# Moving one transposed load behind the first unpacking copies, and splitting four tiles' work on the fourth weight piece

## The chip, the cores and the metric

The kernel runs on one core of one Trainium2 chip. The metric is the device time of one launch in microseconds (us); the time before is the median of three runs.

## The reference

`x` is 16 x 512 x 1024, `w` 1024 x 1024 and `b` 1024, all bf16. Every group of four consecutive rows of `w` keeps, column by column, the elements whose magnitude is at least the second largest of the four; the others become zero. Then the pruned matrix is applied.

```
wg = w.reshape(G, M, D)                      # G = 256 groups, M = 4 rows each
mag = jnp.abs(wg)
order = jnp.argsort(mag, 1)
thr = jnp.take_along_axis(mag, order[:, M - N:M - N + 1, :], 1)     # N = 2
wp = (wg * (mag >= thr)).reshape(D, D)
return jnp.einsum("bsd,df->bsf", x, wp) + b
```

## The kernel before

The 8192 tokens are 64 tiles of 128. Tiles 0 to 6 are "packed": they are multiplied while the weights are still being pruned. Tiles 7 to 13 are "filling" tiles: they keep the matrix engine (PE) busy while later weights are pruned. Tiles 14 and 15 are one small batch, and tiles 16 to 63 run in six batches of eight through a regular loop (L373).

The weights are loaded so that partition p of half g holds the four rows of one group, which is what VectorE (DVE) needs to prune. They come in six pieces: pieces 0 to 3 are 256-column quarters of half g = 0, and pieces 4 and 5 are the two 512-column halves of g = 1. The packed tiles use half 0 in that grouped layout directly, against x tiles whose columns were taken apart in the same way (`xT`, by transposes on PE). Every other tile uses x transposed in natural order, and so needs the pruned weights rearranged into `wp_nat`: four copies from on-chip memory to on-chip memory for each half g and each column half h (`unpack`, L176), all issued from the SyncE queue (SP).

The order of the front part is written out by hand in the string `FRONT`. Each token is one step, and every engine and queue works through its own steps in exactly this order. The tokens that matter here:

- `I.1.0.512`, `I.1.512.1024`: load the two column halves of weight half g = 1 (L71, 512 KB each, SP). The loads of pieces 0 to 3 stand ahead of `FRONT`; pieces 2 and 3 come as one load of 512 KB, `load_w(0, 512, 1024)`.
- `D.0`, `D.1`: `load_fill`, the transposing DMA of the filling tiles' x for half 0 or 1 into `xfill` (L263, SP). `G` (L328) is the same for the packed tiles' half 1, into `xg1`. `L.n` (L275) are the transposing loads of the later batches.
- `U.g.h...`: the four unpacking copies of half g, column half h (L176, SP).
- `A.i`, `P.i`: magnitudes of weight piece i (L120 on DVE; piece 3 on ScalarE, L117), and its pruning on DVE (L133 to L153). Pieces 0 to 3 are masked and pruned in two steps, rows m = 0, 1 of each group first and then m = 2, 3.
- `T.t`, `C.t`: transpose packed tile t on PE, copy the result to `xT` on ScalarE (ACT).
- `M.i.t`: the four matmuls (m = 0 to 3) of piece i for packed tile t (L207). `N.i.t.a.b` does only those of the rows a and b that it names, so that work can start when the first half of a piece is pruned.
- `V.h.t`: ACT copies a finished bank to `stage` (L239). `O.h.t`: DVE adds the second half (L243).
- `X.0.t`: four matmuls of filling tile t on half g = 0, 512 columns wide (L207, reading `xfill` and `wp_nat`). `X.0.7` is the first one, and the first reader of what `D.0` and `U.0.0.0.512` bring. `N.4...` after it need `G` and `U.1.0.0.512`; `X.2...` need `D.1`.

Eight accumulator banks are handed out in turn. Each DMA signals one of eight completion semaphores, also in turn, and waits for the earlier user of that semaphore to have landed.

Of the kernel before, what the change touches and what calls it, by code (L numbers as in the profile page):

```python
# [10 lines left out]
def kernel(  # L11
# [8 lines left out]
    P = 128  # L20
# [7 lines left out]
    B, S, D = x.shape  # L28
# [10 lines left out]
    T, F = 7, 7  # L39
# [230 lines left out]
    def issue_batch(t0, nb):  # L270
# [16 lines left out]


    FRONT = """
        I.1.0.512 D.0 A.0 P.0 W W W W W W W W W w w T.0 T.1 C.0 T.2 T.3 C.1 T.4 C.2 N.0.0.0 N.0.0.1 T.5  # L290
        N.0.1.0 N.0.1.1 N.0.0.2 N.0.0.3 N.0.1.2 N.0.1.3 M.0.2 A.1 C.3 P.1 U.0.0.0.512 I.1.512.1024 G C.4 C.5
        M.0.3 N.0.4.0.1 T.6 C.6 N.0.4.2.3 A.2 M.0.5 M.0.6 P.2 N.1.0.0.1 N.1.1.0.1 A.3
        N.1.2.0.1 N.1.0.2.3 N.1.1.2.3 N.1.2.2.3 V.0.0 M.1.3 V.0.1 M.1.4 V.0.2 M.1.5 M.1.6 V.0.3 V.0.4
        P.3 N.2.0.0.1 V.0.5 N.2.1.0.1 N.2.2.0.1 N.2.3.0.1 N.2.0.2.3 V.0.6 N.2.1.2.3 N.2.2.2.3 N.2.3.2.3 M.2.4 M.2.5 M.2.6 A.4 P.4
        U.1.0.0.512 D.1 N.3.0.0.1 N.3.1.0.1 N.3.0.2.3 V.1.0 N.3.1.2.3 M.3.2 V.1.1 M.3.3 V.1.2 M.3.4 V.1.3 M.3.5 V.1.4
        M.3.6 V.1.5 X.0.7 V.1.6 X.0.8 V.0.7 X.0.9 V.0.8 X.0.10 V.0.9 X.0.11 V.0.10 X.0.12 V.0.11 X.0.13 V.0.12 V.0.13
        A.5 P.5 U.1.1.0.512 U.0.1.0.512 Q L.0 L.1 N.4.0.0 N.4.1.0 N.4.2.0 N.4.3.0 N.4.0.1 N.4.1.1 N.4.2.1
        N.4.3.1 N.4.0.2 N.4.1.2 N.4.2.2 N.4.3.2 N.4.0.3 N.4.1.3 N.4.2.3 N.4.3.3 M.4.4 O.0.0 M.4.5 O.0.1
# [109 lines left out]
```

## Time and profile before

| what | us |
|---|---|
| median of 3 runs (233.39 to 233.41) | 233.39 |
| profiled execution, whole | 234.25 |
| its span in the profile | 232.4 |
| PE busy | 227.2 (98%) |
| VectorE busy | 120.4 (52%) |
| ScalarE busy | 17.1 (7%) |
| regular loop L373 on the closing chain | 72% of the span |
| L207 (packed and filling tiles) on the closing chain | 12% of the span |
| granted TensorE clock | 1.0 |

The span starts with the first instruction of the profiled execution; all times below are microseconds from there. 1.85 us of the profiled execution lie outside the span, and that execution is 0.86 us longer than the median. "Busy" of PE counts pipelined matmuls that overlap: one 256-column matmul is recorded as 273 ns, while the next starts 109 ns after it. DMA shares are the mean busy share of the core's 16 DMA engines; they exceed 1 where packets overlap.

### The profile page before, as it was taken

The page shows a single profiled execution, that of the slowest core. Times are in us where ns is not written, and L with a number is a line of the kernel's source. Part 1 is how long each engine was busy: PE and PEld are TensorE (multiplying, and loading weights), DVE is VectorE, ACT ScalarE, POOL GpSimd, SP SyncE. Part 2 cuts the span into 40 slices and gives each one's busy share as a digit, 9 for nine tenths or more (in the row PEclk, how much of TensorE's full clock was granted, in tenths as well). Part 3 has the DMA queues.
Part 4 walks back from the last instruction along what each step waited for, and adds up shares of the span by engine and source line. Part 5 has one row for each costly group of instructions (what it writes and reads, how often), then busy time and mean ns, then how long its engine had stood idle before and what let it go on. Part 6 is the DMA issues. An engine that isn't in the chain of part 4 may idle for free.

```text
span 232.4 us, 2743 instructions
## 1 busy us (share of the span) xinstructions
PE 227.2 (98%) x1123; PEld 110.3 (47%) x1143; DVE 120.4 (52%) x214; ACT 17.1 (7%) x31; POOL 0.7 (0%) x6
## 2 busy tenths in 40 slices
PE   8989999999999999999999999999999999999995
PEld 4876444444444444444444444444444444444443
DVE  4899987777996244234334334324424424423434
ACT  3677500000000000000000000000000000000000
POOL 1000000000000000000000000000000000000000
DMA  6989999999846203992239922597228991122222
GB/s 212 236 187 206 222 234 177 249 249 305 303 181 258 103 26 112 238 253 97 93 101 206 234 92 93 109 233 199 90 93 175 162 278 36 73 90 90 90 90 93
DMA packets 77612, 38.19 MB, mean 164 GB/s; under 512 B 63648, under 2 KB 69408, under 8 KB 77600
## 3 DMA queue, kind: packets, MB, share of 16 engines
q1 hardware_dynamic: 67952, 20.88, 46.7%
q10 hardware_dynamic: 9648, 17.14, 20.4%
q8 instruction: 9, 0.15, 0.3%
q14 instruction: 3, 0.02, 0.0%
HBM read 3.28 MB, written 16.78 MB: 86 GB/s over the span
## 4 chain that ended last, share of the span: by engine, by line
PE 90%; DVE 3%; DMA 3%; SPq 1%; issue 1%
PE bank L373 72%; PE bank L207 12%; PE bank L267 6%; DMA w<-in_w_dram 3%; SPq L79 1%; DVE w L153 1%; DVE mask L150 1%; SPq L71 0%; DVE o_last L358 0%; DVE hi L133 0%; DVE lo L134 0%; DVE thr L143 0%; DVE mag L120 0%; DVE t L141 0%; DVE t L137 0%
## 5 line engine op out<-in xcount | busy, mean ns | idle before, releaser
L373 PE MATMUL bank<-wp_nat,xTb 128*128 128x512 bf16 x737 | 161.7, 379 | 0.8
L252 DVE TENSOR_TENSOR o_pair<-bank,bias_sb 128x512 bf16<-128x512 f32 x105 | 68.0, 687 | 101.2 <-PE bank L373 95.4
L373 PEld LDWEIGHTS <-xTb 128*128 128x128 bf16 x752 | 73.6, 98 | 88.7
L243 DVE TENSOR_TENSOR stage<-bank,stage 128x512 f32<-128x512 f32 x21 | 13.7, 688 | 2.9 <-PE bank L207 2.8
L207 PE MATMUL bank<-w,xT 128*128 128x256 bf16 x112 | 13.3, 273 | 0.8 <-DVE w L153 0.8
L247 DVE TENSOR_TENSOR o_pair<-stage,bias_sb 128x512 bf16<-128x512 f32 x21 | 13.5, 683 | 0.0
L207 PE MATMUL bank<-wp_nat,xfill 128*128 128x512 bf16 x55 | 12.4, 379 | 0.1
L267 PE MATMUL bank<-wp_nat,xfill 128*128 128x512 bf16 x55 | 12.2, 379 | 0.1
L207 PE MATMUL bank<-wp_nat,xg 128*128 128x512 bf16 x54 | 12.1, 380 | 0.1
L207 PEld LDWEIGHTS <-xT 128*128 128x128 bf16 x112 | 10.7, 98 | 2.7 <-issue 1.1
L239 ACT COPY stage<-bank 128x512 f32<-128x512 f32 x21 | 11.0, 609 | 4.2 <-PE bank L207 4.1
L267 PEld LDWEIGHTS <-xfill 128*128 128x128 bf16 x56 | 5.5, 98 | 6.6
L207 PEld LDWEIGHTS <-xg 128*128 128x128 bf16 x56 | 5.5, 98 | 6.6 <-issue 0.2
L207 PEld LDWEIGHTS <-xfill 128*128 128x128 bf16 x56 | 5.5, 98 | 6.4
L373 PE MATMUL bank<-wp_nat,xTs 128*128 128x512 bf16 x32 | 7.1, 379 | 0.0
L153 DVE TENSOR_TENSOR w<-w,mask 128x512 bf16<-128x512 bf16 (+2 forms) x11 | 5.9, 546 | 0.3
L150 DVE TENSOR_TENSOR mask<-mag,thr 128x512 bf16<-128x512 bf16 (+2 forms) x11 | 5.9, 543 | 0.2
L105 PE MATMUL bank<-const-bfloat16-1.0 128*128 128x512 bf16 (+1 forms) x11 | 4.2, 572 | 0.8 <-PEq L392 0.8
L373 PEld LDWEIGHTS <-xTs 128*128 128x128 bf16 x32 | 3.1, 98 | 3.8
L120 DVE TENSOR_SCALAR mag<-w 128x512 uint16<-128x512 uint16 (+2 forms) x6 | 2.7, 469 | 3.1 <-DMA w<-in_w_dram 3.0
L191 ACT COPY xT<-bank 128x512 bf16<-128x512 bf16 x7 | 3.6, 609 | 2.9 <-PE bank L186 2.9
L267 PE MATMUL bank<-wp_nat,xTb 128*128 128x64 bf16 (+3 forms) x39 | 3.6, 248 | 0.1
(20 smaller groups left out, 27.1 us busy)
## 6 DMA issues: line engine op xcount, KB each, us to landing
out_dram<-o_pair ACTq DMA_DIRECT2D x25, 512.0 KB, 3.6
out_dram<-o_pair ACTq DMA_DIRECT2D x13, 256.0 KB, 3.2
wp_nat<-w SPq DMA_DIRECT2D x16, 128.0 KB, 3.1
w<-in_w_dram SPq DMA_DIRECT2D x3, 512.0 KB, 7.1
xh<-in_x_dram SPq DMA_DIRECT2D x3, 128.0 KB, 4.0
xh<-in_x_dram ACTq DMA_DIRECT2D x1, 256.0 KB, 3.9
xh<-in_x_dram SPq DMA_DIRECT2D x1, 256.0 KB, 3.4
w<-in_w_dram SPq DMA_DIRECT2D x1, 256.0 KB, 4.2
```

Of the source, the lines that this page charges most:

```text
L105: K(nc.tensor.matmul(bank[7][:, :n], lhsT=ones[:, :P], rhs=ones[:, :n], start=True, stop=True))
L120: K(nc.vector.tensor_single_scalar(mag[:, ms].bitcast(u16), w_of(i)[:, ms].bitcast(u16), 0x7FFF, op=Alu.bitwise_and))
L150: K(nc.vector.tensor_tensor(mask[:, ms, c], mag[:, ms, c], tb, op=Alu.is_ge))
L153: K(nc.vector.tensor_tensor(w_of(i)[:, ms, c], w_of(i)[:, ms, c], mask[:, ms, c], op=Alu.mult))
L191: K(nc.scalar.copy(xt[:], src))
L207: K(nc.tensor.matmul(dst, lhsT=lhs, rhs=rhs, start=c0 == 0 and m == 0, stop=c1 == FH and m == 3))
L239: K(nc.scalar.copy(stage[(h, t)][:], bank[own[(h, t)]][:]))
L243: K(nc.vector.tensor_tensor(st, bank[own[(2 + h, t)]][:], st, op=Alu.add))
L247: K(nc.vector.tensor_tensor(get_o(t)[:, f], stage.pop((h, t))[:], bias_sb[:, f], op=Alu.add))
L252: K(nc.vector.tensor_tensor(get_o(t)[:, f], bank[bk][:], bias_sb[:, f], op=Alu.add))
L267: K(nc.tensor.matmul(bank[bk][:, :c1 - c0], lhsT=xN[t][:, kt, :], rhs=wp_nat[h][:, kt, c0:c1], start=kt == 0, stop=kt == KT - 1))
L373: K(nc.tensor.matmul(bank[bks[h]][:], lhsT=xN[t][:, kt, :], rhs=wp_nat[h][:, kt, :], start=kt == 0, stop=kt == KT - 1))
```

## The change

Two edits in `FRONT`; nothing else in the kernel differs. `D.0` goes from second place to a place behind `U.0.0.0.512`. For packed tiles 2 and 3 the fourth piece (i = 3) is split: the first-half matmuls of both go ahead of every second-half matmul of that piece, as those of tiles 0 and 1 already did.

```diff
-        I.1.0.512 D.0 A.0 P.0 W W W W W W W W W w w T.0 T.1 C.0 T.2 T.3 C.1 T.4 C.2 N.0.0.0 N.0.0.1 T.5
-        N.0.1.0 N.0.1.1 N.0.0.2 N.0.0.3 N.0.1.2 N.0.1.3 M.0.2 A.1 C.3 P.1 U.0.0.0.512 I.1.512.1024 G C.4 C.5
+        I.1.0.512 A.0 P.0 W W W W W W W W W w w T.0 T.1 C.0 T.2 T.3 C.1 T.4 C.2 N.0.0.0 N.0.0.1 T.5
+        N.0.1.0 N.0.1.1 N.0.0.2 N.0.0.3 N.0.1.2 N.0.1.3 M.0.2 A.1 C.3 P.1 U.0.0.0.512 D.0 I.1.512.1024 G C.4 C.5
...
-        U.1.0.0.512 D.1 N.3.0.0.1 N.3.1.0.1 N.3.0.2.3 V.1.0 N.3.1.2.3 M.3.2 V.1.1 M.3.3 V.1.2 M.3.4 V.1.3 M.3.5 V.1.4
+        U.1.0.0.512 D.1 N.3.0.0.1 N.3.1.0.1 N.3.2.0.1 N.3.3.0.1 N.3.0.2.3 V.1.0 N.3.1.2.3 N.3.2.2.3 V.1.1 N.3.3.2.3 V.1.2 M.3.4 V.1.3 M.3.5 V.1.4
```

## The prediction

> **What bounds the kernel now.** I read the closing chain first. It ends in PE work without a gap, but its head is a weight load and the pruning on VectorE that waits for it:
>
> ```profile
> 4.10 7.12 DMA w<-in_w_dram
> 11.21 0.02 issue
> 11.24 0.44 DVE mag L120
> ...
> 17.59 0.43 DVE w L153
> 18.03 0.04 issue
> 18.07 3.86 PE bank L207 x29
> 21.93 0.05 issue
> ```
>
> The load of pieces 2 and 3 lands at 11.21; VectorE prunes both pieces without pause; PE goes on at 18.07 and never stops again for long (the profile's 0.8 us in front of L373 is spread over 737 matmuls). What PE loses before 18.07 is therefore lost to the whole. Then the timeline, PE and VectorE, for where it is lost:
>
> ```profile
> 9.06 4.51 PE L207 MATMUL bank<-w,xT 128*128 128x256 bf16 x38
> 14.16 3.71 PE L207 MATMUL bank<-w,xT 128*128 128x256 bf16 x32 [0.59 <-DVE w L153]
> 18.07 2.78 PE L207 MATMUL bank<-w,xT 128*128 128x256 bf16 x24 [0.20 <-DVE w L153]
> 20.68 6.21 PE L207 MATMUL bank<-wp_nat,xfill 128*128 128x512 bf16 x27
> 10.21 0.42 DVE L153 TENSOR_TENSOR w<-w,mask 128x512 bf16<-128x512 bf16 x1
> 11.24 0.43 DVE L120 TENSOR_SCALAR mag<-w 128x1024 uint16<-128x1024 uint16 x1 [0.60 <-DMA w<-in_w_dram]
> ```
>
> PE waits twice for pruned weights, and VectorE itself waits 0.60 us for the load. Matmuls of this shape start every 0.109 us ((2.78 - 0.27) / 23) and are recorded as 0.27, so a wait costs 0.164 us more than the idle time shown: 0.59 + 0.164 = 0.75 us before piece 2 and 0.20 + 0.164 = 0.36 us inside piece 3. The 32 matmuls from 14.16 take 3.71 instead of 31 x 0.109 + 0.27 = 3.65: another 0.06 us, where piece 3 begins (its first half is pruned at 17.22, PE gets there at 14.16 + 28 x 0.109 = 17.21). Sum: 1.17 us. `X.0.7` starts at 20.68.
>
> Last, the SP queue and what the DMA engines do meanwhile (stretches: length, busy of the engines, clock, DMA share, GB/s):
>
> ```profile
> 4.10 1.23 SPq L71 DMA_DIRECT2D w<-in_w_dram  x2
> 5.38 8.38 SPq L263 DMA_TRANSPOSE xfill<-in_x_dram  x1
> 13.89 3.47 SPq L176 DMA_DIRECT2D wp_nat<-w  x4
> 17.41 0.61 SPq L71 DMA_DIRECT2D w<-in_w_dram  x1
> 18.06 5.57 SPq L328 DMA_TRANSPOSE xg<-in_x_dram  x1
> 23.73 2.48 SPq L176 DMA_DIRECT2D wp_nat<-w  x4
> 26.26 3.66 SPq L263 DMA_TRANSPOSE xfill<-in_x_dram  x1
> ```
>
> ```profile
> 2.00:6.50 4.50, 4.50 (x27) 2.83 (x26) 3.17 (x16) 2.33 (x5) 0.00 (x0) 1.00 1.06 321
> 6.50:10.50 4.00, 3.98 (x44) 3.38 (x42) 3.74 (x11) 2.57 (x6) 0.00 (x0) 1.00 1.19 252
> 19.50:20.50 1.00, 1.00 (x12) 0.90 (x10) 1.00 (x3) 1.00 (x4) 0.00 (x0) 1.00 1.01 337
> ```
>
> `D.0` is issued at 5.38, behind the load that VectorE waits for, and holds SP until 13.76. About 1.1 us after that issue the loads slow from 321 to 252 GB/s, though the same kind of weight load reaches 337 at 19.5. `D.0`'s own data moves only at 12.5 to 15.2 (290 GB/s in every half microsecond there). Issue to landing: `D.0` 12.1, `D.1` 5.7, `G` 7.7 us.
>
> **The change part by part.** It adds no instruction; every matmul, copy and DMA stays.
>
> *The weight load without `D.0` behind it.* By 6.5 the loads have moved 321 x 4.5 = 1.44 MB. Up to and with pieces 2 and 3, 1.97 MB are asked for (the KB of the issue list, 15 x 128 KB). The other 0.52 MB take 1.6 us at 337 GB/s, 2.1 at 252: they end at 8.1 to 8.6, and with up to an us for the slowest engine the load lands before 9.6. VectorE is busy until 10.63, so it gains the whole 0.60 us and not more. Bounds: 0 (the load lands at 11.21 whatever stands behind it) and 0.60. I take 0.60, since the rate falls just when `D.0` begins.
>
> In ring order, says the Trainium skill (DMA: Bandwidth & Descriptors, Queues, rings and completion order), each DMA engine takes its descriptors; by that rule a transfer issued later could not delay this load. Row and rule differ here; by the rule this term is 0.
>
> *PE with VectorE 0.60 earlier.* Piece 2 starts at 13.56 instead of 14.16: 0.15 of the 0.75 us stays, since PE itself would be ready at 13.41. Piece 3 starts at 16.67, its 0.06 stays. *Halves:* the second half is pruned at 18.01 - 0.60 = 17.41. Now eight first-half matmuls stand ahead of it instead of four, so PE reaches it at 16.67 + 8 x 0.109 = 17.54: the 0.36 us goes. The first bank copy, `V.1.0`, comes four matmuls later in piece 3 but still about 0.5 us earlier than its 18.48; its reader `X.0.8` comes two us later, so it costs nothing. With both edits `X.0.7` could start at 20.68 - 0.60 - 0.36 = 19.72. The upper bound of the gain is thus 0.96 us.
>
> *`D.0` behind the unpacking copies.* Now SP passes nothing from 5.35 until piece 1 is pruned at 10.63, then issues four copies (2.48 us by the row at 23.73) and `D.0` at about 13.2. It is no longer free: `X.0.7` needs it at 19.72, 6.5 us later. The nearest row is `D.1`, the same transfer behind four such copies: 5.7 us, landing at 18.9, no wait. `G` (7.7 us) stood behind a 512 KB load and would give 20.9; its own old row (12.1) gives 25.3, but 7 us of that were spent behind 1 MB of loads. Against 18.9 speaks one thing the row of `D.1` did not meet, an instruction fetch (queue, packets, MB, share of 16 engines from 15 to 16 us):
>
> ```profile
> q8 instruction: 1, 0.02, 7.3%
> ```
>
> 7.3% of 16 engines is 1.17 us on one engine. The fetches repeat every 27 us with PE's progress, so this one comes at about 14.6, into the last unpacking copy or the start of `D.0`. The transposing phases begin only when the copies ahead have drained (near 28.5 for `D.1`, whose last copy was issued at 25.6: the rate goes from 225 to 286 GB/s within a us), so one late engine can hold back all: up to 1.2 us, landing 18.9 to 20.1. I take 19.9, near the late end, as the fetch falls in that stretch: `X.0.7` at 20.0, a wait of 0.28 us.
>
> *Queue behind `D.0`.* `D.1`'s issue took 3.66 us, so `I.1.512.1024` is issued at 16.9 to 18 (17.41 before; VectorE wants it at 22.9) and `G` at 17.5 to 18.7 (18.06). `U.1.0` then waits for piece 4's pruning, 23.73 - 0.60 = 23.13, lands its first copy 2.8 us later at 25.9 (before: 26.5 for a use at 26.73, so only 0.2 us to spare). PE's `N.4.0.0` wants it at 26.73 - 0.68 = 26.05. This cover is thin: a gain above 0.83 us would meet it. `D.1` lands 0.6 earlier too, at 31.4, for a use at 32.1. `L.n` and the bias have over 5 us.
>
> Sum: 0.60 + 0.36 - 0.28 = 0.68 us, rounded 0.7. The profiled execution is 0.86 us over the median, outside this stretch, so I take the same microseconds off the median: 233.39 - 0.7 = 232.7. Some 0.2% (0.47 us) is what a measurement of this kernel can tell from no change.
>
> **The rivals.** (a) *`D.0` in full time*, by `D.1`'s row: 0.83 to 0.96 us, 232.4 to 232.55. For it: same transfer, same predecessor. Against: the fetch, and `U.1.0`. With the forecast it makes one case, 0.60, range 232.4 to 232.9.
>
> (b) *The load lands at 11.2 anyway*: only the halves help, 233.39 - 0.36 = 233.0. For it: it was queued ahead of `D.0`, behind 1.4 MB. The Trainium skill's rule on ring order, above, makes this case. Against: the falling rate. 0.10.
>
> (c) *`D.0` lands late but not very*, 20.2 to 21.1: between -0.47 and +0.47, about 233.3. For it: the row of `G`, 20.9. Against: `G` waited for a load that itself waited for the copies. 0.13.
>
> (d) *`D.0` becomes the new bound*: PE stands at `X.0.7`, with nothing else in its order to do. The change turns slower once `D.0` lands after 20.68, measurably so after 21.15; every us later costs one. At 22.1, the row of `G` and an engine held for 1.2 us, 234.8; at 25.3, its old row, 238.0. For it: 6.5 us of room where this transfer once took 12.1. Against: it needs 8 us from issue where neither `D.1` nor `G` did. 0.17, with the chance that `U.1.0` slips likewise.
>
> **How the numbers follow.** Faster by over 0.2%: 0.60; within: (b) and (c), 0.23; slower: 0.17. The likeliest case gives 232.7. The range runs from 232.4, the most that the waits allow, to 233.6, which holds (b), (c) and the mildest of (d) (landing by `G`'s row, 20.9 + 0.1 for the start).
>
> **What would show it.** Right: the idle 0.60 of VectorE before L120 near 11 gone, pieces 2 and 3 landed before 10.6, PE's 0.59 down to near nothing and the 0.20 inside piece 3 gone, `D.0` issued at 13.2 in 4 to 5 us, landed before 20.1, and a PE wait on the DMA into `xfill` under 0.4 us. Wrong: VectorE still waiting for the load (b), or a wait of over 0.5 us at `X.0.7` or at L207 on `xg1` (c, d).

## The result and the profile after

The changed kernel takes 234.15 us (median of 9 runs, 233.62 to 234.55) where the kernel before takes 233.41 (nine runs too, 233.36 to 233.88): a ratio of 1.0029, 95% interval 1.0018 to 1.0040. That is 0.74 us slower, clear of no change; 0.7 us faster was forecast, with 232.4 to 233.6 as the range.

The profiled execution of the changed kernel (234.15 us, span 232.4) shows that the closing chain now runs through the SP queue and `D.0` (start, us, what):

```profile
10.65 0.35 DVE mag L120
11.00 0.28 SPq L176
...
11.97 1.37 SPq L176
...
14.03 6.52 DMA xfill<-in_x_dram
20.55 0.05 issue
20.60 24.35 PE bank L207 x112
```

The chain no longer runs through the pruning of pieces 2 and 3. It leaves VectorE when piece 1 is done (at 10.64; the first copy is issued at 10.68, and the row of `mag` above covers part of it), goes through the four unpacking copies on SP, one of which holds the queue for 1.37 us, then through `D.0`, and reaches PE when `D.0` lands. In the timeline of the same execution the forecast's first half is there: VectorE starts piece 2 at 10.57 without a wait (11.24 before), PE waits 0.22 instead of 0.59 us in front of it, and the wait inside piece 3 is gone. All of that is then spent in front of `X.0.7`:

```profile
10.57 0.42 DVE L120 TENSOR_SCALAR mag<-w 128x1024 uint16<-128x1024 uint16 x1
13.48 6.33 PE L207 MATMUL bank<-w,xT 128*128 128x256 bf16 x56 [0.22 <-DVE w L153]
20.60 6.22 PE L207 MATMUL bank<-wp_nat,xfill 128*128 128x512 bf16 x28 [0.78 <-DMA xfill<-in_x_dram]
```

`X.0.7` starts at 20.60, where the first profile of the kernel before had it at 20.68, and the two profiled executions took nearly the same (234.15 and 234.25 us). By the profiles there is no loss; by the medians there is one of 0.74 us. So the first question for the experiments was the profile of before itself.

### The profile page after: what moved, and what is told of

It is laid out like the page before. It is cut to its first block, busy times and chain, and to the rows that moved or that the text cites. A ratio compares the mean times of both kernels' runs of the same rounds, so it can differ in the third digit from the quotient of the medians.

```text
span 232.4 us, 2763 instructions
## 1 busy us (share of the span) xinstructions
PE 227.9 (98%) x1143; PEld 109.6 (47%) x1143; DVE 120.4 (52%) x214; ACT 17.3 (7%) x31; POOL 0.7 (0%) x6
## 3 DMA queue, kind: packets, MB, share of 16 engines
q10 hardware_dynamic: 9648, 17.14, 20.6%
## 4 chain that ended last, share of the span: by engine, by line
PE 90%; DMA 5%; DVE 2%; SPq 2%; issue 0%
PE bank L373 73%; PE bank L207 10%; PE bank L267 6%; DMA xfill<-in_x_dram 3%; DMA w<-in_w_dram 2%; SPq L176 1%; SPq L79 1%; DVE o_last L358 0%; DVE w L153 0%; DVE mag L120 0%; DVE mask L150 0%; SPq L71 0%; DVE hi L133 0%; DVE lo L134 0%; DVE thr L143 0%
## 5 line engine op out<-in xcount | busy, mean ns | idle before, releaser
L207 PE MATMUL bank<-w,xT 128*128 128x256 bf16 x112 | 13.2, 272 | 0.2 <-DVE w L153 0.2
```

Source lines behind the costliest of these rows:

```text
L207: K(nc.tensor.matmul(dst, lhsT=lhs, rhs=rhs, start=c0 == 0 and m == 0, stop=c1 == FH and m == 3))
```

## The experiments

**Two theories.** Theory 1: the profiled execution of before, 0.86 us over its median, had lost that time in front of `X.0.7`, and in a usual execution `D.0`'s late landing is a plain loss. Theory 2: the front part always looks as in that profile, and the change costs somewhere behind it.

**The kernel before, profiled twice more** (no edit).

> The kernel before, unchanged, profiled a second time. Its first profiled execution took 234.25 us, 0.86 more than its median, and there X.0.7 started at 20.68. Theory 1, the first profiled execution was no typical one and its extra 0.86 us lie in front of X.0.7 (the load of pieces 2 and 3 was held up more than usual): an execution near 233.4 shows X.0.7 at 19.7 to 20.1 and VectorE waiting for the load 0 to 0.2 us instead of 0.60. Theory 2, the front part always looks like that and the change costs somewhere behind it: an execution near 233.4 shows X.0.7 at 20.6 to 20.7 again and is shorter elsewhere. Time against itself: 0.

> The kernel before once more, for a third profiled execution: where the load of pieces 2 and 3 lands with D.0 issued right behind it (11.21 and 9.01 so far; 9.90, 10.61 and 9.91 in three kernels without it). If D.0 held the load up, as the prediction said, it lands at 10.5 or later; if its time only varies from execution to execution, 9 to 10.6 is likely, and X.0.7 starts near 19.9.

The second profiled execution took 233.39 us, the third 233.37. Timeline of the second:

```profile
8.68 8.37 PE L207 MATMUL bank<-w,xT 128*128 128x256 bf16 x70
17.25 2.78 PE L207 MATMUL bank<-w,xT 128*128 128x256 bf16 x24 [0.20 <-DVE w L153]
19.86 6.21 PE L207 MATMUL bank<-wp_nat,xfill 128*128 128x512 bf16 x27
```

PE goes through 70 matmuls without the 0.59 us gap, and `X.0.7` starts at 19.86 (19.82 in the third). Against 20.68 that is 0.82 and 0.86 us, nearly the whole difference in time (0.86 and 0.88 us, from 234.25 to 233.39 and 233.37). Theory 1 holds, and the loss of the change reads off directly: 20.60 less 19.86, 0.74 us.

In that execution the load of pieces 2 and 3 took 4.9 us from issue to landing, with `D.0` issued behind it at 5.37, as before (the issue list, stretch 4.05 to 4.2; the columns are output and input, queue, count, KB, us to landing):

```profile
w<-in_w_dram SPq DMA_DIRECT2D x1, 512.0 KB, 4.9
```

In the changed kernel, where no transposing DMA stands behind the load until 14.03, the same list says:

```profile
w<-in_w_dram SPq DMA_DIRECT2D x1, 512.0 KB, 5.8
```

The rate of the loads says the same. For the stretch in which the prediction saw it fall to 252 GB/s with `D.0` behind (last column, GB/s), the second profile of the kernel before has 308 with the same `D.0` behind, and the changed kernel 266 without it:

```profile
6.50:10.50 4.00, 3.98 (x40) 3.25 (x38) 3.83 (x12) 3.29 (x6) 0.00 (x0) 1.00 1.11 308
6.50:10.50 4.00, 3.98 (x41) 3.35 (x39) 3.74 (x11) 3.18 (x7) 0.00 (x0) 1.00 0.81 266
```

**The change undone, one part at a time.** `halves_only`: only the fourth line of the diff; `move_only`: only `D.0`'s place. `halves_again` repeats the first.

```diff
 halves_only, halves_again:
-        N.3.0.0.1 N.3.1.0.1 N.3.0.2.3 V.1.0 N.3.1.2.3 M.3.2 V.1.1 M.3.3 V.1.2
+        N.3.0.0.1 N.3.1.0.1 N.3.2.0.1 N.3.3.0.1 N.3.0.2.3 V.1.0 N.3.1.2.3 N.3.2.2.3 V.1.1 N.3.3.2.3 V.1.2
 move_only:
-        I.1.0.512 D.0 A.0 ... P.1 U.0.0.0.512 I.1.512.1024 G
+        I.1.0.512 A.0 ... P.1 U.0.0.0.512 D.0 I.1.512.1024 G
```

> Only the split of piece 3 for tiles 2 and 3; D.0 stays where it was. Theory 1: the 0.36 us inside piece 3 goes, nothing else: 233.0, 0.1 to 0.4 under the kernel before. Theory 2: the time lost lies behind the front and the split has no part in it: the same 233.0 or, if the split itself is what costs, 234.1.

> The split alone once more, for its time: the first try gave a ratio of 0.9996 (0.9985 to 1.0006) to the kernel before. Theory 1: the 0.36 us inside piece 3 goes but part of it is kept by VectorE's wait or pace in some executions: 0.1 to 0.35 us under the kernel before, 233.1 to 233.6. Rival: no difference at all, ratio 1.000.

> Only D.0 behind the unpacking copies; piece 3 as before. Theory 1: D.0's landing (20.55 in the profile of the changed kernel) sets X.0.7 whatever PE does ahead of it, so this runs like the changed kernel, 234.0 to 234.3, and the split makes no difference to it. Theory 2: if the split is what costs, 233.4.

The split alone measures 0.9996 (0.9985 to 1.0006) and 0.9998 (0.9983 to 1.0013): medians 0.15 and 0.16 us under the kernel before, not more than the runs' own spread. Their fastest executions (233.09 and 233.07) are 0.28 and 0.29 us under the fastest of the kernel before in the same rounds (233.37 and 233.36), so the split does give something where nothing else is late. The profiled execution of `halves_again` (234.34) shows how it is lost: `X.0.7` starts at 19.97, but PE then waits at `N.4.0.0`. The profile gives a bank copy on ACT as the releaser; the first unpacking copy of `U.1.0`, issued at 23.95, right behind `G`, lands at about the same time (2.6 to 2.9 us after its issue).

```profile
26.85 3.40 PE L207 MATMUL bank<-wp_nat,xg 128*128 128x512 bf16 x15 [0.67 <-ACT stage L239]
```

The move alone measures 1.0033 (1.0021 to 1.0045), 234.45 us, as expected from Theory 1: `D.0` is issued at 14.20, takes 6.7 us, and `X.0.7` follows it at 20.91. The loss belongs to the move.

A second look at the changed kernel:

> The changed kernel once more, for a second profiled execution: D.0 lands at 20.2 to 21, X.0.7 follows within 0.1 us, and everything behind runs without a gap; the load of pieces 2 and 3 at 9 to 10.6, as in the kernels where D.0 follows it.

It took 234.28 us; `D.0` issued at 14.03, 6.6 us to landing, `X.0.7` at 20.69.

**The wait taken away.** In `x0_no_wait` the filling tiles' matmuls on half g = 0 read `xT` instead of `xfill`; all DMAs stay.

```diff
-                lhs, rhs = xN[t][:, 4 * g + m, :], wp_nat[h][:, 4 * g + m, c0:c1]
+                lhs, rhs = (xN[t][:, 4 * g + m, :] if g else xT[t - T][:, m, :]), wp_nat[h][:, 4 * g + m, c0:c1]
```

> The changed kernel with every DMA where it is, but the filling tiles' first four matmuls (X.0.7 to X.0.13) read the packed tiles' xT instead of xfill, so that they do not depend on D.0 (this multiplies other x rows for that part). Theory 1 (PE's wait for D.0 is the whole loss): X.0.7 starts at 19.4 to 19.8, at 19.54 by the changed kernel's own matmuls (the last one ahead of the wait started at 19.54); 233.0 to 233.4, that is 0.7 to 1.1 us under the changed kernel and 0 to 0.4 under the kernel before. Rival (D.0's traffic or the held queue behind it costs too): 233.8 to 234.1, with a wait at N.4.0.0 for G or the copies of U.1.0.

233.72 us, 1.0005 (0.9991 to 1.0018) of the kernel before: 0.17 us over the kernel before in the same rounds, where the changed kernel was 0.74 over it, but less of a gain than Theory 1 alone expected. In the profiled execution (234.03, one of the longer) `X.0.7` starts early, at 19.77, but the next stage then waits, as the rival had it:

```profile
19.77 6.21 PE L207 MATMUL bank<-wp_nat,xT 128*128 128x512 bf16 x28
26.54 3.83 PE L207 MATMUL bank<-wp_nat,xg 128*128 128x512 bf16 x17 [0.57 <-DMA wp_nat<-w]
```

The copies of `U.1.0` were issued at 23.64, right behind `G`, where the kernel before (second profile) issued them at 22.80 as soon as VectorE was done; here VectorE was done at 23.04. So most of the loss is PE's wait for `D.0`, and under it lies a second wait: what stands behind `D.0` on SP is just late for `N.4.0.0`, and the first wait hides it. This second wait is not the move's alone, since `halves_again` waits there too, with `D.0` in its old place.

**`D.0` left out** (`no_d0`).

```diff
-        I.1.0.512 A.0 ... U.0.0.0.512 D.0 I.1.512.1024 G
+        I.1.0.512 H A.0 ... U.0.0.0.512 I.1.512.1024 G
+        elif k == "H":
+            K(nc.gpsimd.memset(xfill[:, 0:4, :], 0.0))
```

> The changed kernel with D.0's load left out: the first half of xfill is cleared by GpSimd instead, so the filling tiles' first four matmuls multiply zeros. Theory 1 (D.0 behind the unpacking copies lands too late, and that is the whole loss): no wait of PE in front of X.0.7, which starts at 19.4 to 19.8 instead of 20.60; 233.0 to 233.4, 0.7 to 1.1 under the changed kernel and 0 to 0.5 under the kernel before. Rival (the loss comes from elsewhere on the SP queue, the held third copy or later loads): 234.1, as the changed kernel. It also shows the load of pieces 2 and 3 with nothing transposing behind it: by the prediction's reading it lands before 9.6, by ring order at 9 to 10.6 as in the other runs.

234.00 us, 1.0016 (1.0007 to 1.0024). This run tells less than it was meant to, because the replacement costs time of its own (timeline, GpSimd and VectorE):

```profile
1.24 3.08 POOL L326 MEMSET xfill<- 128x3584 bf16 x1
3.29 1.39 DVE L120 TENSOR_SCALAR mag<-w 128x512 uint16<-128x512 uint16 x2 [2.42 <-DMA w<-in_w_dram]
```

While GpSimd clears 3584 columns, until 4.32, VectorE's first two instructions take 1.39 us instead of 0.52 in the changed kernel (the first alone 1.19, the second, which starts after the clear, 0.28), and the pruning behind them starts 0.87 us later. No wait for a DMA stands in front of `X.0.7` (20.34), which is all it shows. The load took 5.7 us with no transposing DMA behind it.

**`D.0` one place later** (`late_d0`).

```diff
-        U.0.0.0.512 D.0 I.1.512.1024 G
+        U.0.0.0.512 I.1.512.1024 D.0 G
```

> The changed kernel with D.0 one place further back, behind I.1.512.1024 too. Theory 1: D.0's phase starts after that load has drained, near 18.3, and it lands at 21.9 to 22.5; X.0.7 follows it at once, 1.3 to 1.9 us later than in the changed kernel: 235.4 to 236.0. Rival: D.0's landing is not what sets the end; 234.1 again.

Four runs: 235.15, 236.10, 238.35 and 239.43 us; the ratio to the kernel before is 1.0086 (1.0062 to 1.0111) without the longest. The mechanism is as expected, `X.0.7` follows the landing of `D.0` at once. In the first two runs the mean granted clock stayed at 1.000, and they are 1.0 and 2.0 us over the changed kernel, near the 1.3 to 1.9 expected. In the other two it was 0.993 and 0.984, and the price is higher. The profiled execution is the third: `D.0` takes 8.0 us and lands at 23.1, `X.0.7` comes 2.5 us later than in the changed kernel, and the time is 4.2 us longer. The rest is PE's clock (timeline; then the stretch 24.55 to 27.54, granted clock ahead of the last two columns):

```profile
23.11 1.25 PE L207 MATMUL bank<-wp_nat,xfill 128*128 128x512 bf16 x5 [3.42 <-DMA xfill<-in_x_dram]
```

```profile
24.55:27.54 2.99, 2.99 (x8) 1.03 (x8) 2.89 (x6) 0.99 (x3) 0.00 (x0) 0.50 1.06 236
```

About 1 us after PE starts again behind 3.42 us without work, the granted clock falls to 0.50. In half-microsecond stretches it is 0.77 from 24.0, 0.50 from 24.5 to 27.5 and 0.82 from 27.5, together some 3.4 us at half clock, which loses 1.7 us: all of the rest.

**`D.0` ahead of the copies, but held until the load has landed** (`gate`, with the split).

```diff
-        I.1.0.512 D.0 A.0
+        I.1.0.512 H D.0 A.0
+        elif k == "H":
+            K(nc.gpsimd.tensor_copy(xfill[:, 0, 0:16], w_gh[(0, 1)][:, 0, 0:16]))
```

> The changed kernel, but D.0 back ahead of the unpacking copies in SP's order and held until the load of pieces 2 and 3 has landed: GpSimd copies 16 columns of that load into xfill, which D.0 then overwrites. D.0 is issued near 10 instead of 5.4 or 14.0. Theory 1: the load is not disturbed, D.0 lands near 15 to 16, the copies of U.0.0 near 17 to 18, nothing is late, X.0.7 starts at 19.7 to 19.8: 0.7 to 0.9 us under the changed kernel, 233.2 to 233.5. Theory 2: like the changed kernel, 234.1.

234.26 us (233.45 to 235.43), 1.0030 (1.0013 to 1.0046): no gain over the changed kernel. The profiled execution, 235.29, is one of the longest of the twelve, so its waits are not those of a usual one. In it `X.0.7` comes at 19.67 as expected, but `D.0`, issued at 10.21, takes 7.4 us to land instead of the 5 to 6 expected, and keeps SP until 15.46; `G` and the copies of `U.1.0` follow at 18.83 and 24.88, and PE waits for them instead, once, at `N.4.0.0` (waits: us, times, longest):

```profile
PEld L207 <- DMA xg<-in_x_dram: 2.1, 1, 2.1
PE bank L207 <- DMA wp_nat<-w: 1.6, 1, 1.6
```

Why `D.0` took so long shows in the list of queues. No load is ahead of it any more after 11.3, its packets begin to move near 11.6, and then they all but stop, from 13.0 to 14.75, right behind an instruction fetch (packets, MB, share of 16 engines, in 12 to 13, 13 to 14 and 15 to 16 us):

```profile
q8 instruction: 1, 0.02, 11.0%
q1 hardware_dynamic: 5, 0.00, 11.3%
q1 hardware_dynamic: 1135, 0.29, 127.7%
```

The fetch's 11.0% of 16 engines is 1.76 us, if one engine carries it; without such a stop `D.0` would have taken about 5.6 us, the time of `D.1`. This is one trace, so that the fetch stopped it is likely and not shown.

**A queue with more room** (`early_i`, twice): the split, `D.0` in its old place, and the last weight load moved up ahead of it, so that `G` follows the unpacking copies directly.

```diff
-        I.1.0.512 D.0 A.0 ... U.0.0.0.512 I.1.512.1024 G
+        I.1.0.512 I.1.512.1024 D.0 A.0 ... U.0.0.0.512 G
```

> The split, D.0 ahead of the unpacking copies as in the kernel before, and the last weight load, I.1.512.1024, moved up in front of D.0, so that no load stands between the unpacking copies and G. Theory 1: D.0 lands about 1.6 us later than in the kernel before (16.7 to 19), still ahead of X.0.7; G and U.1.0 come earlier and the executions in which N.4.0.0 waited for them vanish: 233.0 to 233.3, 0.1 to 0.4 under the kernel before. Rival (D.0's room is used up): a wait at X.0.7, 233.8 or more.

> The split with the last weight load moved up ahead of D.0, once more, for its time and for a profiled execution near its fastest; the first try gave 0.9981 (0.9968 to 0.9995) of the kernel before, and its profiled execution (233.96) was one of its slow ones, with a wait of 0.34 us for the unpacking copies at X.0.7. Theory 1: 233.0 to 233.3, and an execution near 233.05 shows PE without a wait from the first packed tiles on, X.0.7 at 19.4 to 19.6. Rival (the first ratio was luck): ratio 1.000.

233.21 us against 233.55, 0.9981 (0.9968 to 0.9995), and 233.19 against 233.45, 0.9991 (0.9981 to 1.0001). That is 0.34 and 0.26 us under the kernel before, though the second interval just reaches 1, and some 0.9 us under the changed kernel. How much of it is the split and how much the load moved up was not separated. Both of its profiled executions (233.96 and 233.62) are above its median, so the expected execution without a wait was not seen. In both, the copies of `U.1.0` are issued at 23.18, as soon as VectorE is done and well after `G` has left SP; in the first, PE waits 0.34 us behind `X.0.7` for an unpacking copy, so the copies of `U.0.0` are the next thing to come late.

## Why the prediction was wrong

The profiled executions side by side. The load of pieces 2 and 3 and `D.0` are given from issue to landing; `D.0` lands, and `X.0.7` starts, at the times shown.

| kernel | load, us | D.0, us | D.0 lands | X.0.7 | profiled us |
|---|---|---|---|---|---|
| before, first profile | 7.1 | 12.1 | 17.5 | 20.68 | 234.25 |
| before, second | 4.9 | 9.8 | 15.2 | 19.86 | 233.39 |
| before, third | 5.6 | 10.5 | 15.9 | 19.82 | 233.37 |
| halves_only | 5.3 | 10.1 | 15.6 | 19.79 | 233.34 |
| halves_again (waits again at `N.4.0.0`) | 6.8 | 11.7 | 17.1 | 19.97 | 234.34 |
| changed | 5.8 | 6.5 | 20.55 | 20.60 | 234.15 |
| changed, second | 6.4 | 6.6 | 20.6 | 20.69 | 234.28 |
| move_only | 6.5 | 6.7 | 20.9 | 20.91 | 234.45 |

*The base of the sum: the step that turned the sign.* "The profiled execution is 0.86 us over the median, outside this stretch, so I take the same microseconds off the median." Nothing had been read for that; 0.82 of the 0.86 us lie in this stretch. The 0.59 us wait that the change was credited with removing is not there in a usual execution, and the 0.20 inside piece 3 is there in the second profile but not in the third. From `X.0.7` at 19.84 (mean of the two usual ones), with PE able to reach it at 19.65 in the changed kernel (19.53 in `late_d0`), both edits could have given 0.2 to 0.3 us, not 0.96.

*The load's 0.60 us.* "I take 0.60, since the rate falls just when `D.0` begins." With `D.0` right behind it the load took 7.1, 4.9, 5.6, 5.3 and 6.8 us, mean 5.9; in the seven kernels and executions without it, 5.8, 6.4, 6.5, 6.5, 5.7, 5.8 and 5.8 (changed twice, `move_only`, `x0_no_wait`, `no_d0`, `late_d0`, `gate`), mean 6.1. On the average there is no such effect, and the rate falls after 6.5 without `D.0` too. One coincidence in one trace was taken for a cause. By the rule quoted against it, ring order (the Trainium skill, DMA: Bandwidth & Descriptors, Queues, rings and completion order), this term is 0; these twelve traces agree on the average. Why the load varies stays open, and so does whether `D.0` widens its spread (4.9 to 7.1 us with it, 5.7 to 6.5 without).

*`D.0`'s landing, the term that was mis-sized.* Forecast 13.2 + 5.7 and up to 1.2, taken as 19.9; measured 20.55 to 20.9. The four copies were priced at 2.48 us from `U.1.0`'s row, with the row of the very same copies, 3.47, in the same fence; they took 3.31:

```profile
10.68 3.31 SPq L176 DMA_DIRECT2D wp_nat<-w  x4
```

The instruction fetch was foreseen, but tied to PE's progress, "every 27 us", and set at 14.6. The later fetches of the first profile do come some 27 us apart (at 33, 60, 86 and 114), but this one, at 15, does not fit that row. In thirteen of the fourteen profiles it comes with the third unpacking copy (1.2 to 1.9 us of issue instead of 0.60), wherever that stands; only in `gate` does it fall on `D.0`, and there all four copies take 0.6. The list of queues has it in 15 to 16 us in the first profile of before, in 12 to 13 in the second, and in 11 to 12 here:

```profile
q8 instruction: 1, 0.02, 7.8%
```

From issue to landing `D.0` took 6.5 to 6.8 us in this place (6.8 in `x0_no_wait`), 0.8 to 1.1 more than the row of `D.1`. The extra lies in its last packets: in the changed kernel the full rate, 287 to 292 GB/s, ends near 19.0 and `D.0` lands 1.5 us later, while `D.1` in the first profile of before lands some 0.6 us after its full rate ends. What holds the last packets was not settled. So PE loses 0.94 us at `X.0.7` (1.05 from start to start, less 0.11), not 0.28. The sum by the right terms is 19.65 + 0.95 - 19.84 = 0.76 us slower; 0.74 was measured.

*The range.* Its top, 233.6, was said to hold the mildest of (d). By the prediction's own numbers that case gives 233.39 + 21.0 - 20.68 = 233.7, and (c) runs to 233.9. The measured 234.15 lies above these too.

*What held.* The split removes the wait inside piece 3 where there is one, PE reaches `X.0.7`'s place at 19.65 (19.72 said; in part luck, as the load's 0.60 us came from the load's own spread), and SP's queue behind `D.0` falls where it was put: `I.1.512.1024` at 17.67, `G` at 18.30, `U.1.0` at 23.05 (said 16.9 to 18, 17.5 to 18.7, 23.13). The thin cover of `N.4.0.0` was named, and `x0_no_wait` shows what is under it. Rival (d) had the mechanism, a wait for `D.0` with nothing else for PE to do; its turning point, put at 20.68, is 19.84, and "every us later costs one" holds only while the wait is short (`late_d0`).

## What to carry to other kernels

Before a wait in a profile is counted as a gain, compare that execution's own time with the median: if it is longer, the wait may be the very thing that made it longer, and a second profile costs less than a wrong forecast. Moving a transfer later is priced by its landing against its first reader, with the row of the same instructions in the same place on the queue, and then by what stands behind it. When the wait moved from `X.0.7` to `N.4.0.0` in two experiments, the queue as a whole was the bound there, and the one version that came out ahead, by 0.1 to 0.2%, gave it back room instead of changing who is late.

## What the runs showed of the hardware

A wait of 3.42 us on PE was followed, 1 us later, by some 3.4 us at half the granted clock (`late_d0`), while 0.78 us (the changed kernel) and 1.63 us (`gate`) were followed by full clock. The Trainium skill (TensorE: Matmul & The Clock Gate, Part 1) gives about 3.4 us without work as the point where the clock is halved; `late_d0` agrees. The same size of transposing DMA took 5.7 to 6.0 us from issue to landing as `D.1`, 6.5 to 6.8 as `D.0` behind the first copies, 8.0 behind a 512 KB load (`late_d0`) and 9.8 to 12.1 behind all the weight loads. It was not only what stood ahead of it: in `gate` it took 7.4 with the last load ahead of it landed at 11.3, hardly moving for 1.75 us behind an instruction fetch. An instruction fetch and a longer issue on SP came together in thirteen profiles. And a GpSimd clear of 3584 columns in `no_d0` went with VectorE's first two instructions taking 1.39 us instead of 0.52.
